# Loading k and q one head at a time, with whole 128-token blocks on the partitions, in an attention and expert kernel

## The chip, the cores and the metric

The kernel runs on one NeuronCore of one Trainium2 chip. The metric is the device time of one execution in microseconds (us). PE is the matrix engine, DVE the vector engine, ACT the scalar engine, POOL the GpSimd engine, and SP the engine whose queue issues most DMAs.

## The reference

Attention with a block-causal mask, followed by a mixture of experts:

```python
B, H, S, D = 8, 8, 576, 64
scores = q @ k.transpose(0, 1, 3, 2) / sqrt(D)
scores = where(pos_q // 64 >= pos_k // 64, scores, -1e9)
attn = softmax(scores); out = attn @ v
x = out.transpose(0, 2, 1, 3).reshape(B * S, H * D)        # 4608 x 512
# 4 groups of 4 experts: the group by argmax(x @ w_group), then the expert in it
y[n] = g_w[n] * e_w[n] * (relu(x[n] @ w1[g, e]) @ w2[g, e])
```

All inputs and the output are float32.

## The kernel before

The attention stage takes two heads of one batch at a time, a pair; there are 32 pairs. Its order is written out by hand: `period(x)` goes through the list ORDER, in which a token names a piece of work (K transposes of k and q, k copies of their high parts, l their low parts, W shifts, P and p copies on POOL, S scores, D row maxima, E exponentials, T and t transposes of the probabilities and their copies, V and v the product with v), and each token belongs to pair x, x+1 or an earlier one. Every engine executes its instructions in the order in which they were issued, and waits in it for semaphores. One pass of the list begins on PE with `K1 V0 K0 S5 K2 S6 T4`.

A pair goes like this. `load` (lines 136 to 147) brings k and q of two heads from HBM to SBUF, with token 4p+c on partition p: one DMA of 256 KB for each of k and q, and one of 32 KB for each one's last 64 tokens (the tail). `prep` transposes them on PE: K0 for k, K1 for q, four transposes each into one PSUM tile (line 174), and K2 for the two tails, two transposes of 64 rows (line 178). Because partition p holds tokens 4p to 4p+3, the four transposed blocks hold interleaved tokens, and `parts` writes them to their places with every fourth word:

```python
f = lambda t: t[:, BLK * z:BLK * z + 512].rearrange("r (p c) -> r c p", c=4)
yield nm, f(hi), f(lo), ps.rearrange("r (c p) -> r c p", c=4)
```

`high` (tokens k0 on ACT, k1 on DVE, k2 on ACT; lines 305 to 311) rounds them to fp32r; `low` (l0, l1, l2 on DVE, line 200) stores the difference. Then three DMAs from SBUF to SBUF on SP's queue (`shift`, line 234; W0, W1, W2) bring rows to the other half of the partitions. W2 overwrites what W0 and W1 read, so it waits until they have landed. Scores with even numbers of the next period read what W2 writes; the first of them is S6. W0 needs k0, k1 and k2, W1 needs l1 and l2.

On SP's queue the order of one period is: the three loads of v (lines 155 and 156), W0, W1, in some periods stores of tokens (line 683), W2, and at the period's end the loads of k and q for the pair three further on. Buffers for k and q are two each, for v three. PSUM tiles of the transposes are taken in turn from two pools of two; T4 takes the buffer that K1 had.

The experts follow after about 400 us: tokens are gathered, weights loaded and split, and two products are formed for each expert slot.

Of the kernel before, what the change touches and what calls it, by code (L numbers as in the profile page):

```python
# [8 lines left out]
F32 = mybir.dt.float32  # L9
# [8 lines left out]
P = 128  # L18
D = 64
S = 576  # L20
BLK = 64
# [55 lines left out]
class Attention:  # L77
# [58 lines left out]
    def load(self, i):  # L136
        nc = self.nc
        b, pr = divmod(i, 4)
        h0 = 2 * pr
        out, src = {}, dict(k=self.k, q=self.q)  # L140
        for nm in "kq":
            out[nm] = self.nat.tile([P, 10, D], F32, tag="nat" + nm, name=f"nat{nm}{i}")
            nc.sync.dma_start(out[nm][:, 0:8, :].rearrange("p (c a) d -> p c a d", a=2),
                              src[nm][b, h0:h0 + 2, 0:512, :].rearrange("a (p c) d -> p c a d", c=4))
        for nm in "kq":
            nc.sync.dma_start(out[nm][0:64, 8:10, :], src[nm][b, h0:h0 + 2, 512:576, :].rearrange("a p d -> p a d"))
        self.lds[i] = out

    def load_v(self, i):
# [9 lines left out]
    def prep(self, i, n):  # L159
        nc = self.nc  # L160
        r = self.rs.setdefault(i, {})
        ld = self.lds[i]
        if "qk" not in r:
            x, t, r["zq"] = r["qk"] = self.qk[i % 2]
            r["ql"], r["q"], r["k"] = x[:, 0, :], [x[:, 1, :], t[:, 0, :]], [x[:, 2, :], t[:, 1, :]]
            r["kl"], r["qm"], r["kn"] = [t[:, 2, :], t[:, 3, :]], [t[:, 4, :], t[:, 5, :]], t[:, 6, :]
            r["qx"] = t[:, 4:6, :].rearrange("p z s -> p (z s)")[:, S - BLK:S + BLK]
        ident = self.c["ident"]
        ps = self.psT(f"tp{i}_{n}")
        r["ps", n] = ps  # L170
        if n < 2:
            x = ld["kq"[n]]
            for c in range(4):
                nc.tensor.transpose(out=ps[:, c * P:(c + 1) * P],  # L174
                                    in_=x[:, 2 * c:2 * c + 2, :].rearrange("p a d -> p (a d)"), identity=ident)
        else:
            for z in range(2):
                nc.tensor.transpose(out=ps[:, 64 * z:64 * z + 64], in_=ld["kq"[z]][0:64, 8:10, :].rearrange("p a d -> p (a d)"),
                                    identity=ident[0:64, 0:64])

    def parts(self, i, n):
        r = self.rs[i]
        ps = r["ps", n]
        for z, nm in enumerate("kq"):
            hi, lo = r[nm][0], r["ql" if nm == "q" else "kn"]
            if n == z:
                f = lambda t: t[:, BLK * z:BLK * z + 512].rearrange("r (p c) -> r c p", c=4)
                yield nm, f(hi), f(lo), ps.rearrange("r (c p) -> r c p", c=4)
            elif n == 2:
                w = slice(0, BLK) if z else slice(512, S)  # L190
                yield nm, hi[:, w], lo[:, w], ps[:, 64 * z:64 * z + 64]
# [1118 lines left out]
```

## Time and profile before

| | |
|---|---|
| median of 3 runs | 921.68 us (920.98 to 924.41) |
| span of the profiled execution, first to last instruction | 926.3 us (4.6 above the median; it has no other time of its own) |
| busy share of the span: PE, DVE, ACT, POOL | 95%, 65%, 58%, 26% |
| PE busy in the stretch 200 to 246 us | 45.9 of 46 |
| DVE and ACT busy in the same stretch | 42.7 and 39.5 of 46 |
| chain that ended last, by engine | PE 73%, DMA 13%, DVE 6%, issue 3%, ACT 2%, POOL 2% |
| largest DMA line of the chain | qk<-qk, 8% |

Busy time of PE counts from the start of an instruction to its modelled end; consecutive ones overlap. The chain follows the last instruction back, at each step to what released it. "Issue" of a DMA is the time on the queue of the engine that starts it; its landing comes later. An engine's idle time is put down to the semaphore that came last.

### The profile page before, as it was taken

To read this page: it belongs to the slowest core of one execution; us is meant where nothing else is said; L and a number is where in the kernel's file an instruction comes from. 1 tells how busy PE (TensorE), PEld (TensorE's weight loads), DVE (VectorE), ACT (ScalarE), POOL (GpSimd) and SP (SyncE) were. 2 spreads that over 40 slices of the span, in tenths; PEclk is the share of its full clock that TensorE was granted. 3 is DMA by queue.
4 is the path that set the end of the run, shared out by engine and by line. 5 is a ranking of instruction groups with operands and counts; after the bars stand their busy time and mean duration, and the time that the engine had idled before them with its cause. 6 is when DMAs were issued, how large, how long until landed. Compare 5 with 4: busy or idle time off the path is not lost.

```text
span 926.3 us, 17222 instructions
## 1 busy us (share of the span) xinstructions
PE 876.0 (95%) x5681; PEld 723.1 (78%) x5681; DVE 601.0 (65%) x1390; ACT 538.2 (58%) x1374; POOL 240.5 (26%) x462
## 2 busy tenths in 40 slices
PE   7899999989997999979989999999999999999996
PEld 5677777777776777757767887887888888988885
DVE  6767988869896888956863435346354465655562
ACT  5888888858885888857333325343243354645451
POOL 5343141312323131314150212321121123122011
PEclk7999999989998999989998999999999999999999
DMA  5777877967788677877442545554564567655671
GB/s 123 147 157 174 181 140 170 162 142 175 140 179 147 151 159 151 183 76 205 100 130 83 161 154 205 173 192 157 169 209 147 151 192 231 209 186 167 175 242 41
DMA packets 192842, 149.03 MB, mean 161 GB/s; under 512 B 127302, under 2 KB 158022, under 8 KB 192752
## 3 DMA queue, kind: packets, MB, share of 16 engines
q1 hardware_dynamic: 184704, 128.17, 56.6%
q0 software_dynamic: 8048, 19.76, 6.2%
q8 instruction: 46, 0.75, 0.3%
q14 instruction: 44, 0.36, 0.2%
HBM read 100.88 MB, written 19.70 MB: 130 GB/s over the span
## 4 chain that ended last, share of the span: by engine, by line
PE 73%; DMA 13%; DVE 6%; issue 3%; ACT 2%; POOL 2%; SPq 0%; POOLq 0%; ACTq 0%; DVEq 0%
PE h L977 17%; PE y L1022 16%; DMA qk<-qk 8%; PE s L254 7%; PE tp L297 7%; PE o L329 6%; PE y L1027 4%; DMA wh<-in_moe_w_dram 2%; PE s L263 2%; PE tp L174 2%; PE h L972 2%; PE ye L1022 2%; DVE nm L268 1%; DVE qk L200 1%; PE xp L945 1%
## 5 line engine op out<-in xcount | busy, mean ns | idle before, releaser
L278 ACT ACTIVATE pb<-s,nm 128x384 f32<-128x384 f32 (+4 forms) x288 | 157.7, 557 | 50.1 <-DVE nm L268 47.0
L268 DVE TENSOR_REDUCE nm<-s 128x1 f32<-128x384 f32 (+4 forms) x288 | 137.7, 512 | 51.4 <-PE s L254 50.3
L254 PE MATMUL s<-qk 128*128 128x384 f32 (+3 forms) x512 | 138.5, 364 | 28.4 <-DMA qk<-qk 19.9
L977 PE MATMUL h<-xt,wh 128*128 128x264 f32 (+6 forms) x704 | 155.3, 312 | 0.0
L929 DVE TENSOR_TENSOR wl<-raw,wh 128x512 fp32r<-128x512 f32 x192 | 123.5, 684 | 10.6 <-ACT wh L928 10.3
L977 PEld LDWEIGHTS h<-xt,wh 128*128 128x128 f32 x704 | 119.4, 188 | 9.1
L309 ACT COPY pt<-tp 128x512 f32<-128x512 f32 (+1 forms) x224 | 113.5, 549 | 16.1 <-PE tp L297 14.9
L297 PE MATMUL tp<-ident,pb 128*128 128x128 f32 x800 | 119.7, 279 | 0.5
L254 PEld LDWEIGHTS s<-qk 128*128 128x128 f32 x512 | 82.2, 198 | 36.1 <-issue 16.9
L977 PE MATMUL h<-xt,wl 128*128 128x264 f32 (+6 forms) x352 | 109.4, 311 | 0.0
L928 ACT CAST wh<-raw 128x512 fp32r<-128x512 f32 x192 | 109.1, 620 | 0.2
L297 PEld LDWEIGHTS tp<-ident,pb 128*128 128x128 f32 x800 | 93.4, 143 | 18.5 <-PE s L254 6.5
L1022 PE MATMUL y<-wh,hring 128*128 128x512 f32 x306 | 107.2, 401 | 0.0
L994 DVE SCALAR_TENSOR_TENSOR hring<-h,hring 128x32 fp32r<-128x32 f32 (+7 forms) x112 | 35.7, 356 | 105.9 <-ACT hring L990 102.6
L329 PE MATMUL o<-pt,vb 128*64 128x320 f32 (+4 forms) x896 | 100.6, 362 | 1.2 <-DVE xte L953 1.0
L990 ACT ACTIVATE hring<-h 128x288 fp32r<-128x288 f32 (+7 forms) x62 | 28.9, 466 | 121.5 <-PE h L977 53.7
L329 PEld LDWEIGHTS o<-pt,vb 128*64 128x64 f32 x896 | 60.3, 137 | 41.0 <-ACT pt L309 2.8
L1048 POOL DMA_INDIRECT out_dram<-ys,ids x40 | 42.4, 1059 | 189.7 <-DVE ys L1044 177.8
L200 DVE SCALAR_TENSOR_TENSOR qk<-tp,qk 128x64 fp32r<-128x64 f32 (+1 forms) x128 | 78.3, 651 | 6.9 <-ACT qk L309 5.7
L892 POOL DMA_INDIRECT xg<-xd,ids x40 | 41.6, 1041 | 104.8 <-DMA ids<-tab 36.4
L977 PEld LDWEIGHTS h<-xt,wl 128*128 128x128 f32 x352 | 66.2, 188 | 1.2
L1022 PEld LDWEIGHTS y<-wh,hring 128*128 128x128 f32 x306 | 57.6, 188 | 11.8
(229 smaller groups left out, 1437.6 us busy)
## 6 DMA issues: line engine op xcount, KB each, us to landing
raw<-in_moe_w_dram SPq DMA_DIRECT2D x96, 512.0 KB, 3.8
qk<-qk SPq DMA_DIRECT2D x93, 288.0 KB, 3.6
natk<-in_k_dram SPq DMA_DIRECT2D x32, 256.0 KB, 4.0
natq<-in_q_dram SPq DMA_DIRECT2D x32, 256.0 KB, 4.7
vb<-in_v_dram SPq DMA_DIRECT2D x64, 128.0 KB, 3.4
xd<-xns SPq DMA_DIRECT2D x32, 256.0 KB, 5.8
wh<-in_moe_w_dram SPq DMA_DIRECT2D x16, 512.0 KB, 4.8
rawe<-in_moe_w_dram SPq DMA_DIRECT2D x8, 512.0 KB, 7.0
```

Source lines behind the costliest of these rows:

```text
L200: nc.vector.scalar_tensor_tensor(out=lo, in0=ps, scalar=0.125 if nm == "q" else 1.0, in1=hi.bitcast(F32), op0=ALU.mult, op1=ALU.subtract)
L254: nc.tensor.matmul(st[:, 0, 0:w], lhsT=r[a][z][:, q0:q0 + P], rhs=r[c][z][:, 0:w], start=x == 0, stop=x == 1)
L268: self.nc.vector.tensor_reduce(out=r["nm"][:, t:t + 1], in_=r["s", t], op=ALU.max, axis=AX.X if t < 8 else AX.XY, negate=True)
L278: nc.scalar.activation(reg, r.pop(("s", t)), AF.Exp, bias=r["nm"][:, t:t + 1], accum_out=self.sms[b][:, pr, t % 2, t // 2:t // 2 + 1])
L297: nc.tensor.transpose(out=o, in_=pb[:, POFF[x] + j * P:POFF[x] + (j + 1) * P], identity=self.c["ident"])
L309: self.nc.scalar.copy(dst, src)
L329: nc.tensor.matmul(o[64 * a:64 * a + 64, BLK * (t - b0):n], lhsT=r["v"][:, a, j, :], rhs=p[:, a], start=x == 0, stop=x == len(pcs) - 1, ti ...
L928: nc.scalar.copy(h[:, sl], s["raw", u][:, sl])
L929: nc.vector.tensor_tensor(out=l[:, sl], in0=s["raw", u][:, sl], in1=h[:, sl].bitcast(F32), op=ALU.subtract)
L977: nc.tensor.matmul(o, lhsT=ww[:, dc, f], rhs=rr[:, dc, t], start=dc == 0 and x == 0, stop=dc == 3 and x == 2)
L1022: nc.tensor.matmul(y[c][0:n], lhsT=hh, rhs=w, start=k == 0 and x == 0, stop=k == 7 and x == 2)
L1048: i = nc.gpsimd.indirect_dma_start(out=self.out, out_offset=bass.IndirectOffsetOnAxis(ap=s["ids"][0:n, c, 0:1], axis=0), in_=ys[0:n], in_o ...
```

## The change

The loads of k and q are made one head at a time, 128 KB each, with token 128c+p on partition p, so that each transposed block holds 128 consecutive tokens. The tails of k and of q go to partitions 0 to 63 and 64 to 127 of the same tile, and one transpose of 128 rows replaces the two of 64. The copies of `parts` become unbroken. The tile of q has 8 instead of 10 rows of 64.

```diff
-        for nm in "kq":
-            out[nm] = self.nat.tile([P, 10, D], F32, tag="nat" + nm, name=f"nat{nm}{i}")
-            nc.sync.dma_start(out[nm][:, 0:8, :].rearrange("p (c a) d -> p c a d", a=2),
-                              src[nm][b, h0:h0 + 2, 0:512, :].rearrange("a (p c) d -> p c a d", c=4))
-        for nm in "kq":
-            nc.sync.dma_start(out[nm][0:64, 8:10, :], src[nm][b, h0:h0 + 2, 512:576, :].rearrange("a p d -> p a d"))
+        for nm, n in (("k", 10), ("q", 8)):
+            out[nm] = self.nat.tile([P, n, D], F32, tag="nat" + nm, name=f"nat{nm}{i}")
+            for a in range(2):
+                nc.sync.dma_start(out[nm][:, a:8:2, :], src[nm][b, h0 + a, 0:512, :].rearrange("(c p) d -> p c d", p=P))
+        for z, nm in enumerate("kq"):
+            nc.sync.dma_start(out["k"][64 * z:64 * z + 64, 8:10, :],
+                              src[nm][b, h0:h0 + 2, 512:576, :].rearrange("a p d -> p a d"))
...
-            for z in range(2):
-                nc.tensor.transpose(out=ps[:, 64 * z:64 * z + 64], in_=ld["kq"[z]][0:64, 8:10, :].rearrange("p a d -> p (a d)"),
-                                    identity=ident[0:64, 0:64])
+            nc.tensor.transpose(out=ps[:, 0:P], in_=ld["k"][:, 8:10, :].rearrange("p a d -> p (a d)"), identity=ident)
...
-                f = lambda t: t[:, BLK * z:BLK * z + 512].rearrange("r (p c) -> r c p", c=4)
-                yield nm, f(hi), f(lo), ps.rearrange("r (c p) -> r c p", c=4)
+                w = slice(BLK * z, BLK * z + 512)
+                yield nm, hi[:, w], lo[:, w], ps
```

## Rows read from the trace of the kernel before

**Rows 1.** Timeline of PE: start us, us, engine line op names [idle before, releaser]
```profile
35.03 0.70 PE L254 MATMUL s<-qk 128*128 128x512 f32 x2 [0.57 <-ACT qk L309]
...
402.49 1.19 PE L254 MATMUL s<-qk 128*128 128x512 f32 x2 [5.62 <-DMA qk<-qk]
```

**Rows 2.** Chain of the stretch 36 to 72 us: start us, us, what
```profile
38.94 4.32 DMA qk<-qk
...
43.40 3.27 DMA qk<-qk
...
46.81 0.71 PE s L254 x2
```

**Rows 3.** Timeline of SP's queue, one period from its loads on
```profile
20.20 0.63 SPq L143 DMA_DIRECT2D natk<-in_k_dram  x1
20.92 0.99 SPq L143 DMA_DIRECT2D natq<-in_q_dram  x1
21.97 0.94 SPq L146 DMA_DIRECT2D natk<-in_k_dram  x1
22.96 0.61 SPq L146 DMA_DIRECT2D natq<-in_q_dram  x1
23.61 1.15 SPq L155 DMA_DIRECT2D vb<-in_v_dram  x2
24.80 0.60 SPq L156 DMA_DIRECT2D vb<-in_v_dram  x1
25.51 1.25 SPq L234 DMA_DIRECT2D qk<-qk  x2
```

**Rows 4.** Timeline of SP's queue, the last period of this kind
```profile
385.61 0.60 SPq L156 DMA_DIRECT2D vb<-in_v_dram  x1
386.32 1.25 SPq L234 DMA_DIRECT2D qk<-qk  x2
```

**Rows 5.** Waits of SP's queue, 20 to 440 us: total us, times, longest us
```profile
SPq L234 <- ACT qk L311: 8.1, 9, 1.4
```

**Rows 6.** Timeline of SP's queue, the longest issue of a load
```profile
182.49 4.99 SPq L146 DMA_DIRECT2D natk<-in_k_dram  x1
```

**Rows 7.** DMA issues by line: count, KB each, median us to landing
```profile
vb<-in_v_dram SPq DMA_DIRECT2D x64, 128.0 KB, 3.4
```

**Rows 8.** Chain of the stretch 108 to 154 us
```profile
108.10 0.27 PE tp L178 x2
...
117.49 0.46 PE tp L174 x4
```

**Rows 9.** Line 178 by form: count, duration ns min/median/max, first and last start
```profile
L178 PEldq EVENT_SEMAPHORE  x31: 51/51/51, 11.3 to 395.3; - x31
```

**Rows 10.** Groups by form: count, busy us, mean ns, idle before, releasers
```profile
L200 DVE SCALAR_TENSOR_TENSOR qk<-tp,qk 128x512 fp32r<-128x512 f32 x64 | 70.1, 1096 | 6.9 <-ACT qk L309 5.7 <-ACT qk L311 0.2
...
L309 ACT CAST qk<-tp 128x512 fp32r<-128x512 f32 x32 | 34.8, 1087 | 7.8 <-PE tp L174 7.2 <-DMA vb<-in_v_dram 0.5
...
L952 ACT CAST xt<-xp 128x512 fp32r<-128x512 f32 x25 | 14.5, 586 | 29.6 <-PE xp L945 29.6
...
L994 DVE SCALAR_TENSOR_TENSOR hring<-h,hring 128x512 fp32r<-128x512 f32 x7 | 4.8, 692 | 13.6 <-ACT hring L990 13.6
```

**Rows 11.** Timeline of all engines around T4 of one period
```profile
203.43 1.10 DVE L200 SCALAR_TENSOR_TENSOR qk<-tp,qk 128x512 fp32r<-128x512 f32 x1
...
204.64 0.31 PEld L297 LDWEIGHTS tp<-ident,pb 128*128 128x128 f32 x3 [0.41 <-PE s L254]
```

**Rows 12.** Chain of the stretch 0 to 37 us
```profile
7.04 1.15 ACT qk L311
...
8.21 1.40 DVE qk L200 x3
...
13.77 1.08 DVE qk L200
```

**Rows 13.** Timeline of POOL around two loads into one tile
```profile
50.87 1.22 POOL L455 DMA_DIRECT2D wcat<-in_moe_w_expert_dram  x2
```

## The prediction

> **What bounds the kernel now.** I read the page's chain first (table above): PE holds 73% of it, and the largest wait by far is DMA qk<-qk, the SBUF-to-SBUF shifts of the attention stage. The change touches only that stage, the first 400 us of the span; the experts after it are PE's work and stay as they are. So I went on to PE's idle time there. PE stands idle visibly in thirteen of the 31 periods, always ahead of the first 512-wide score matmul S6; the first and the last of these are in [rows 1]. The releaser named in the first is an ACT copy, but S6 reads what the third shift (W2) writes. The chain of one of the early stretches says the same [rows 2]: two shifts land at 43.26, W2 is issued at 43.40 and lands 3.27 later, and S6 starts 0.14 behind it. So a period is paced either by PE's own work or by the landing of W2, and the next question is what makes W2 late.
>
> The SP queue answers that [rows 3]. It is in order, and between one W2 and the next W0 stand the loads of k and q, the loads of v and at times a store of tokens. In the shown period W0 goes out at 25.51, 0.11 behind the end of the last v load (24.80 + 0.60). It does so, within 0.11 us of the queue coming free, in 20 of 31 periods; [rows 4] has the last of them. In these the issue times on SP are part of the loop W0, W1, landing, W2, loads, W0. In nine others W0 waited instead for the ACT copy k2, 8.1 us in all [rows 5]: there the compute engines set the pace and SP has slack.
>
> **The change part by part.** *Issues on SP.* Two loads of 256 KB become four of 128 KB; the tails stay two. Today the block takes 23.61 - 20.20 = 3.41 us [rows 3]. The v load already has the new form (128 KB, one head, token 128c+p on partition p): two of them take 24.80 - 23.61 = 1.19, gap included. Four cost 2.38, two tails at 23.61 - 22.96 = 0.65 cost 1.30, two changes of tile 0.14: 3.82 us, or 0.41 more per period. Both ends: at 1.15 for a pair and 0.61 for a tail without gaps, 3.52, so +0.11; at the natk price (20.92 - 20.20 = 0.72) for each half and 0.99 for the first tail, 4.52, so +1.1. I take 0.41, since the v rows are the same operation. Queued behind are the v loads, the stores and W0; W0 delays W1, these W2, and W2 S6. In five of the 20 periods the first tail's issue stands for over 2 us, the longest in [rows 6]: the queue is stuck there on earlier transfers and two more issues should vanish in it. That leaves 15 x 0.41 = **+6.2 us**. The loads are used two periods later, so that their own landing is late by a little costs nothing.
>
> The bytes and the 256-byte pieces are unchanged; a half load lands 3.4 us after its issue [rows 7]. The rows also show that landings overlap: v loads leave 0.6 us apart though each takes 3.4. The Trainium skill, "SBUF — State Buffer", section on the DMA setup-cost knee, says that every transfer pays roughly 2 us that doesn't shrink with its bytes, and to use the largest single transfer; by that rule, if the fixed parts added up in the queue, 62 more DMAs would be an estimated 124 us. The rows just read speak against paying it in series, so the sum goes without it.
>
> *PE.* The two 64-row transposes of the tails take 0.27 of the chain; four full ones take 0.46, so one takes 0.115 [rows 8]: 0.155 saved per period. Against that, K0 and K1 must each wait for two loads instead of one. These landed long before, so only the semaphore instruction counts, 51 ns each [rows 9], if PE's sequencer has no room for it. I take 0.10 (bounds 0.05 and 0.155).
>
> *ACT and DVE copies.* Today they write every fourth word: l0 and l1 on DVE take 1096 ns, k0 on ACT 1087. Unbroken ones of the same size and operation, from PSUM, take 692 (hring) and 586 (xt) [rows 10]. So each DVE instruction saves 0.40 and k0 0.50; with k1 on DVE that is 1.2 us of DVE and 0.5 of ACT per period, some 38 and 16 us in all. Nearly all of it is hidden: by PE where PE paces, by the SP loop where W2 paces. It comes out in two places. The transposes T4 reuse the PSUM buffer of K1, and their weight load sits idle for 0.41 until 204.64, just after l1's end at 203.43 + 1.10 = 204.53 [rows 11]. With l1 done 0.4 to 0.8 earlier that wait goes; part of it lies under S6's stream, so I take 0.25 (bounds 0 and 0.41). And k2 ends earlier, so W0 moves along in the periods that wait for it.
>
> PE-paced periods thus gain 0.10 + 0.25 = 0.35. In the 20 SP-paced ones it only becomes waiting. In the nine where W0 waits for k2 the whole loop moves: 9 x 0.35 = **-3.2 us** (bounds -0.5 and -5.0).
>
> *Start.* Until the loop runs, the copies are serial [rows 12]: ACT 1.15, then DVE 1.40 for l1 and the tails, and before the first row maxima of the next pair the DVE copy k1 and its l1 (1.08). Savings 0.5 + 0.4 + 0.4 + 0.4 = **-1.7 us**. The last halves of the second pair's loads are issued some 1.5 us later than its natq is today; if they bind, only the last 0.8 remains. If the next period's k1 and l1 count too, 2.5. I take 1.7, since the data of the first two pairs is the same.
>
> Sum: 6.2 - 3.2 - 1.7 = +1.3 us, 0.14%. The profiled execution spans 926.3 us, 4.6 above the median of 921.68; its durations are applied as differences, so the forecast is 921.68 + 1.3 = **923.0 us**. Runs of before differ by 3.4 us; 0.5%, 4.6 us, is about what can be told from no change.
>
> **The rivals.** *No change (chance 0.53, 923.0, own range 917.1 to 926.2):* small gains of the compute engines against small losses on SP.
>
> *Slower, by SP issues (0.18, about 930):* each half costs what natk costs today and the first tail stays at 0.99. Halfway to that, +0.9 per period, 15 x 0.9 = 13.5, less 4.9, is +8.6. For it: k and q issues are dearer than v's now. Against: they carry twice the pieces. It decides from about +0.63 per period on (9.5 - 4.9 = 4.6).
>
> *Faster (0.18, about 916.5):* the 0.99 of natq and 0.94 of the tail are what long lists of pieces cost the next issue, and shorter lists give it back. Then +0.11 per period is +1.7, PE's full 0.56 in nine periods is -5.0, the start -1.7 to -2.5: -5.0 to -5.8. For it: the long issues stand directly behind the 256 KB loads. Against: the instruction itself seems to cost 0.5 to 0.6 whatever its size, so six are six.
>
> *The stalls move (0.04 each way, about 917 or 928):* now and then a shift lands so late that PE is idle for up to 5.62 [rows 1]. The loop's phase moves by a us or so; one such stall more or fewer is about 5.
>
> *The halves wait for each other (0.03, about 1130):* the two heads of one tile now lie in alternating slots; if the second load is held until the first has landed, each period has two waits of 3.4 us on SP [rows 7], 31 x 6.8 = 211. Against: on POOL's queue two loads into interleaved columns of one tile go out in 1.22 us together [rows 13]. The setup rule of the Trainium skill named above would be a milder form of this case.
>
> **How the numbers follow.** Faster 0.18 + 0.04 = 0.22; same 0.53; slower 0.18 + 0.04 + 0.03 = 0.25. The range leaves out the serial case and the tails of the others: low 916.5, high 930.0.
>
> **What would show it.** The load block of SP in an unhindered period: 3.8 us against 3.41; below 3.55 the faster rival is right, above 4.05 the slower. k0 near 590 ns, l0 and l1 near 690, and k1 about 0.4 shorter. One transpose of the tails, and no idle weight load ahead of T4. PE's waits for the shifts should grow in number and total (thirteen visible ones now), W0 behind SP's last load in more than 20 periods. The first row maxima of the second pair, which follow the l1 of 13.77 [rows 12], about 1.7 us earlier. Wrong it would be if PE waited for something other than W2, if the halves landed later than v's 3.4, or if the periods paced by k2 did not shrink.

## The result, and the profile after

The change makes the kernel slower: 931.24 us median (926.0 to 935.82) against 920.61 (916.78 to 926.16) for the kernel before on the same chip, a ratio of 1.0135 with a 95% interval of 1.0105 to 1.0165. On another chip it was 927.61 against 911.88, ratio 1.0167 (1.0138 to 1.0195). The forecast was 923.0 with a range from 916.5 to 930.0.

The profiled execution of after took 926.08 us, five below its median. That of before, on which the prediction rests, spans 926.3 us; after took 1.8 more than its span of 924.3, so by the same difference before took an estimated 928, more than any of its ten timed runs here. The two spans therefore say nothing about the change, and before was profiled a second time (913.5 us, below).

The load block first. The timeline of SP's queue in after, one unhindered period, answers to [rows 3] (columns: start us, us, engine, line, operation, names, count):

```profile
104.07 1.55 SPq L144 DMA_DIRECT2D natk<-in_k_dram  x2
105.67 1.33 SPq L144 DMA_DIRECT2D natq<-in_q_dram  x2
107.05 0.63 SPq L146 DMA_DIRECT2D natk<-in_k_dram  x1
107.72 0.62 SPq L146 DMA_DIRECT2D natk<-in_q_dram  x1
108.39 1.14 SPq L156 DMA_DIRECT2D vb<-in_v_dram  x2
109.58 0.61 SPq L157 DMA_DIRECT2D vb<-in_v_dram  x1
110.29 2.07 SPq L233 DMA_DIRECT2D qk<-qk  x2
```

From the first half of k to the first load of v it is 108.39 - 104.07 = 4.32; the median over the periods is 4.10, with most at 4.07 to 4.11. Before it was 3.41 in [rows 3], with a median of 3.45. W0 goes out directly behind SP's last load in 26 of the 30 periods.

The copies answer to [rows 10]. Groups of after by form (count, busy us, mean ns, idle before with releasers):

```profile
L199 DVE SCALAR_TENSOR_TENSOR qk<-tp,qk 128x512 fp32r<-128x512 f32 x64 | 43.9, 686 | 6.0 <-ACT qk L308 4.8 <-ACT qk L310 0.2
...
L308 ACT CAST qk<-tp 128x512 fp32r<-128x512 f32 x32 | 19.2, 601 | 6.0 <-PE tp L175 5.3 <-DMA natq<-in_q_dram 0.2 <-DMA vb<-in_v_dram 0.2
```

1096 and 1087 ns became 686 and 601. In the chain of the start, the l1 that stood at 13.77 [rows 12] now begins at 12.56:

```profile
12.56 0.69 DVE qk L199
13.25 0.47 DVE nm L267
```

So the compute engines got what the change promises. The page of after shows where it went (busy times; then the chain that ended last by engine and by line):

```profile
PE 864.5 (94%) x5649; PEld 721.3 (78%) x5649; DVE 572.2 (62%) x1390; ACT 522.8 (57%) x1374; POOL 239.8 (26%) x462
...
PE 73%; DMA 17%; DVE 4%; issue 4%; SPq 1%; ACT 1%; POOL 0%; POOLq 0%; DVEq 0%; ACTq 0%
PE h L976 17%; PE y L1021 16%; DMA qk<-qk 14%; PE s L253 7%; PE tp L296 7%; PE o L328 6%; PE y L1026 4%; PE s L262 3%; PE h L971 2%; PE tp L175 2%; PE ye L1021 2%; DMA wh<-in_moe_w_dram 2%; PE xp L944 2%; PE xn L672 2%; PE he L976 1%
```

The shifts, qk<-qk, are 14% of the chain against 8% before. To see in which periods, I count a period from the start of K1 on PE to the next K1: thirty, the first from about 9 us on. With four pairs to a batch, the stores of tokens and four of a batch's five token scatters (indirect DMAs of POOL into the table, Z1, Z2, Z3, Z0 in ORDER, 8 bytes a row) come at the end of periods 10, 14, 18, 22 and 26; periods 11, 15, 19, 23 and 27 lie behind them. All times in us, one profiled execution each:

| kernel | first period | the five behind a batch | the other 24 | K1 of period 31 starts |
|---|---|---|---|---|
| before, first profile | 11.9 | 82.7 | 290.6 | 394.2 |
| before, second profile | 12.0 | 75.0 | 287.9 | 383.8 |
| after, first profile | 9.9 | 94.2 | 281.8 | 394.8 |
| after, second profile | 10.0 | 95.4 | 282.0 | 396.4 |

Between the two second profiles (913.5 and 926.97 us, on two chips on which before takes 912) the change gains 2.0 in the first period and 5.9 in the 24, and loses 20.4 in the five: 12.6 in all by period 31. It wins in the ordinary periods and loses in five places. The sizes are those of single executions: the five of before differ by 7.7 us between its two profiles, and against the first one the loss is 11.5 to 12.7. The win in the 24 leans on the stalls, too: when these are taken away ("After without the scatters", below), the 24 take 290.0.

One of the five, in after: SP's queue; POOL's scatters; the chain; PE's timeline with idle time before an instruction; and the windows of the period and two parts of it (us; busy us with counts of PE, its weight loads, DVE, ACT and POOL; granted clock of PE; DMA share; GB/s).

```profile
129.08 0.60 SPq L233 DMA_DIRECT2D qk<-qk  x1
129.77 1.55 SPq L144 DMA_DIRECT2D natk<-in_k_dram  x2
131.38 1.14 SPq L144 DMA_DIRECT2D natq<-in_q_dram  x2
132.56 2.33 SPq L146 DMA_DIRECT2D natk<-in_k_dram  x1
134.93 2.57 SPq L146 DMA_DIRECT2D natk<-in_q_dram  x1
```

```profile
124.77 1.02 POOL L801 DMA_INDIRECT tab<-pay,pi  x1 [0.17 <-POOL mark L800]
...
128.63 0.96 POOL L801 DMA_INDIRECT tab<-pay,pi  x1 [0.23 <-issue]
```

```profile
129.08 8.73 DMA qk<-qk
```

```profile
137.95 1.19 PE L253 MATMUL s<-qk 128*128 128x512 f32 x2 [5.11 <-DMA qk<-qk]
```

```profile
128.82:150.78 21.96, 15.71 (x106) 12.10 (x106) 9.94 (x21) 11.46 (x34) 2.93 (x5) 0.84 0.84 127
128.82:138.00 9.18, 2.93 (x22) 1.79 (x21) 2.47 (x5) 3.78 (x13) 1.76 (x4) 0.87 1.02 95
138.00:142.00 4.00, 4.00 (x14) 3.37 (x15) 1.55 (x4) 1.15 (x3) 1.17 (x2) 0.50 0.81 171
```

W2 goes out at 129.08, half a us behind the issue of the fourth scatter, and lands 8.73 later; an unhindered one takes 3.4 to 3.6 in the chain of this profile. Meanwhile the DMA engines are busy throughout (1.02) but move only 95 GB/s. PE waits 5.11 us in one piece for it, and then runs 4 us at the lower of its two clock levels (granted clock 0.50, 1.2 GHz): S6's two matmuls take 1.19 instead of 0.70. The queue behind W2 is stuck as well (2.33 and 2.57 for 32 KB tails, otherwise 0.63).

### The profile page after: what moved, and what is told of

It is laid out like the page before. It is cut to its first block, busy times and chain, and to the rows that moved or that the text cites. A ratio compares the mean times of both kernels' runs of the same rounds, so it can differ in the third digit from the quotient of the medians.

```text
span 924.3 us, 17206 instructions
## 1 busy us (share of the span) xinstructions
PE 864.5 (94%) x5649; PEld 721.3 (78%) x5649; DVE 572.2 (62%) x1390; ACT 522.8 (57%) x1374; POOL 239.8 (26%) x462
## 4 chain that ended last, share of the span: by engine, by line
PE 73%; DMA 17%; DVE 4%; issue 4%; SPq 1%; ACT 1%; POOL 0%; POOLq 0%; DVEq 0%; ACTq 0%
PE h L976 17%; PE y L1021 16%; DMA qk<-qk 14%; PE s L253 7%; PE tp L296 7%; PE o L328 6%; PE y L1026 4%; PE s L262 3%; PE h L971 2%; PE tp L175 2%; PE ye L1021 2%; DMA wh<-in_moe_w_dram 2%; PE xp L944 2%; PE xn L672 2%; PE he L976 1%
## 5 line engine op out<-in xcount | busy, mean ns | idle before, releaser
L267 DVE TENSOR_REDUCE nm<-s 128x1 f32<-128x384 f32 (+4 forms) x288 | 141.5, 516 | 83.2 <-PE s L253 64.2
L253 PE MATMUL s<-qk 128*128 128x384 f32 (+3 forms) x512 | 134.9, 360 | 34.6 <-DMA qk<-qk 28.7
L928 DVE TENSOR_TENSOR wl<-raw,wh 128x512 fp32r<-128x512 f32 x192 | 123.5, 684 | 10.6 <-ACT wh L927 10.3
L308 ACT COPY pt<-tp 128x512 f32<-128x512 f32 (+1 forms) x224 | 113.1, 550 | 16.2 <-PE tp L296 11.5
L296 PEld LDWEIGHTS tp<-ident,pb 128*128 128x128 f32 x800 | 95.3, 143 | 14.3 <-DVE tmp L710 3.4
L1021 PE MATMUL y<-wl,hring 128*128 128x512 f32 x153 | 60.5, 395 | 0.0
```

The lines of the kernel that those rows point to most:

```text
L253: nc.tensor.matmul(st[:, 0, 0:w], lhsT=r[a][z][:, q0:q0 + P], rhs=r[c][z][:, 0:w], start=x == 0, stop=x == 1)
L267: self.nc.vector.tensor_reduce(out=r["nm"][:, t:t + 1], in_=r["s", t], op=ALU.max, axis=AX.X if t < 8 else AX.XY, negate=True)
L296: nc.tensor.transpose(out=o, in_=pb[:, POFF[x] + j * P:POFF[x] + (j + 1) * P], identity=self.c["ident"])
L308: self.nc.scalar.copy(dst, src)
L928: nc.vector.tensor_tensor(out=l[:, sl], in0=s["raw", u][:, sl], in1=h[:, sl].bitcast(F32), op=ALU.subtract)
L1021: nc.tensor.matmul(y[c][0:n], lhsT=hh, rhs=w, start=k == 0 and x == 0, stop=k == 7 and x == 2)
```

## The experiments

Ratios are to the kernel before on the same chip, with a 95% interval. Line numbers follow each kernel.

### The issues

**One DMA a tensor in the new layout.** The kernel after, but:

```diff
-            for a in range(2):
-                nc.sync.dma_start(out[nm][:, a:8:2, :], src[nm][b, h0 + a, 0:512, :].rearrange("(c p) d -> p c d", p=P))
+            nc.sync.dma_start(out[nm][:, 0:8, :], src[nm][b].rearrange("h s d -> (h s) d")[h0 * S:h0 * S + 1024, :]
+                              .rearrange("(c p) d -> p c d", p=P))
```

> The changed kernel with k and q again in one 256 KB DMA each (four issues per period as before), the tails and the unbroken copies as changed. For the address pattern's sake the second head's tokens are read 64 too early, so this kernel computes other scores with the same amount of work. Theory (the two added issues per period lengthen SP's loop): the load block falls back from 4.08 to about 3.4 us, the periods that wait for k2 or PE stay at 10.9, and the time is 5 to 9 us below before (ratio 0.990 to 0.995). Rival (the pattern of 128 consecutive tokens, or the token scatter's stalls, cost the time): still 8 to 12 us above before (1.009 to 1.013).

0.996 (0.9931 to 0.9989). The timeline of SP's queue has four issues again, and the block is 3.47 long:

```profile
100.09 0.55 SPq L143 DMA_DIRECT2D natk<-in_k_dram  x1
100.69 1.09 SPq L143 DMA_DIRECT2D natq<-in_q_dram  x1
101.82 1.03 SPq L146 DMA_DIRECT2D natk<-in_k_dram  x1
102.89 0.62 SPq L146 DMA_DIRECT2D natk<-in_q_dram  x1
103.56 1.27 SPq L156 DMA_DIRECT2D vb<-in_v_dram  x2
```

The same layout, copies and tails gain 0.4% with two issues fewer. The five periods take 83.7, the other 24 279.8: against after, 10.5 and 2.0 less. The 83.7 are still 8.7 above the second profile of before, though no issue was added, and 1.0 above the first.

**The split alone.** The kernel before with one head a DMA, still token 4p+c, copies with every fourth word, two tail transposes:

```diff
-            nc.sync.dma_start(out[nm][:, 0:8, :].rearrange("p (c a) d -> p c a d", a=2),
-                              src[nm][b, h0:h0 + 2, 0:512, :].rearrange("a (p c) d -> p c a d", c=4))
+            for a in range(2):
+                nc.sync.dma_start(out[nm][:, a:8:2, :], src[nm][b, h0 + a, 0:512, :].rearrange("(p c) d -> p c d", c=4))
```

> The kernel before with nothing but the split: k and q one head a DMA, token 4p+c on partition p as before, strided copies and two tail transposes kept. Theory (issues on SP): all of the loss and none of the gains, 10 to 18 us above before (1.011 to 1.020), load block near 4.1 us. Rival (pattern of 128 consecutive tokens or the shared tail is what costs): same as before within 0.3%.

1.0268 (1.0226 to 1.031), above the range expected; the block is 4.37, the five periods take 87.4, the other 24 297.0. Without the fast copies the issues cost 12.4 us in the five and 9.1 in the 24, against the second profile of before.

**Two more issues with nothing in them.** The kernel before plus:

```diff
+        extra = self.nat.tile([1, 2, D], F32, tag="extra", name=f"extra{i}")
+        for a in range(2):
+            nc.sync.dma_start(extra[:, a, :], src["k"][b, h0 + a, 0:1, :])
```

> The kernel before with its own layout, its two 256 KB loads and its two tail transposes, and two more loads of 256 bytes each per period, into a tile that nothing reads, issued on SP behind the tails. If the issues themselves are the cost (the instruction stands on SP whatever its bytes): the load block grows from 3.4 us to about 4.5 (two times 0.55), W0 stands directly behind SP's last load in over 25 of 30 periods, and the time is 1.5 to 3 per cent above before, as with the split alone (1.027). If the cost came with the splitting of the bytes (more but shorter lists, later landings), these 31 KB in all cost nothing: block below 3.8, ratio below 1.005.

1.0214 (1.0169 to 1.0259). SP's queue in one period:

```profile
105.07 0.63 SPq L143 DMA_DIRECT2D natk<-in_k_dram  x1
105.80 1.00 SPq L143 DMA_DIRECT2D natq<-in_q_dram  x1
106.84 0.77 SPq L146 DMA_DIRECT2D natk<-in_k_dram  x1
107.66 0.61 SPq L146 DMA_DIRECT2D natq<-in_q_dram  x1
108.32 0.74 SPq L149 DMA_DIRECT2D extra<-in_k_dram  x2
```

Two loads of 256 bytes stand 0.74 us on SP, less than the 1.1 expected, and cost 2.1%. W0 goes out directly behind SP's last load in 20 periods, not in over 25; seven waits of the shifts on SP, 3.7 us in all, are put down to loads of k and q that had to land. The bytes and the shape of the pieces are not the cost; the number of DMAs issued is. Against the second profile of before the five periods take 12.3 more and the other 24 4.1 more: most of the loss sits behind the batches here too.

**The shared tail transpose alone.** The kernel before with the tails of after and their one transpose:

> The kernel before with the shared tail transpose alone: both tails in one tile, one 128-row transpose, loads and copies of the main part as before. Theory: SP's block stays at 3.4 us, a PE-paced period shortens by 0.1 to 0.2 us, the time by 0 to 3 us (0.997 to 1.000). Rival (a tail loaded to partitions 64 to 127 lands later or costs DMA time): above before by 0.3% or more.

0.9946 (0.9911 to 0.9981), better than expected. On PE's timeline the transposes of the tails and S6 in the second profile of before, then in this kernel:

```profile
93.23 0.27 PE L178 MATMUL tp<-ident,natk 64*128 64x64 f32 x1
93.34 0.22 PE L178 MATMUL tp<-ident,natq 64*128 64x64 f32 x1
93.49 0.73 PE L254 MATMUL s<-qk 128*128 128x512 f32 x2
```

```profile
93.01 0.27 PE L178 MATMUL tp<-ident,natk 128*128 128x128 f32 x1
93.04 0.71 PE L253 MATMUL s<-qk 128*128 128x512 f32 x2
94.07 0.52 PE L296 MATMUL tp<-ident,pb 128*128 128x128 f32 x3 [0.32 <-DVE qk L199]
```

S6 starts 0.03 after the start of the one transpose, not 0.26 after that of the first of two, and K1 to S6 takes 2.21 instead of 2.53. T4 then waits 0.32 for the slow l1, so a PE-paced period stays at 11.5: this saving needs the fast copies to come out. What the kernel gains lies elsewhere: 2.5 us in the five periods (72.5) and 2.2 in the other 24 (285.7), with PE waiting 8.2 us in four places for the shifts instead of 10.1 in six. Both differences are smaller than those between the two profiles of before (7.7 and 2.7).

### Moving the loads of v

**After with the v loads behind W1.** SP waits there for W0 and W1 to land anyway:

```diff
-        if 0 <= x - 1 < N:
-            self.load_v(x - 1)
+        vdone = False
...
             self.token(x - lag(tok), tok, N)
+            if not vdone and tok == ("W", 1):
+                vdone = True
+                if 0 <= x - 1 < N:
+                    self.load_v(x - 1)
```

> The changed kernel with the three loads of v moved on SP's queue from ahead of W0 to behind W1, where the queue stands waiting for W0 and W1 to land. Theory (SP's loop paces): 1.8 us leave the loop, W0 again waits for k2 in most periods, periods without router work near 10.9 us, and the time is 10 to 25 us below the changed kernel, 3 to 15 below before (0.984 to 0.997). Rival (the stalls after the token scatter pace, or the transfers themselves): no better than the changed kernel, 1.008 or more.

0.9971 (0.9937 to 1.0005), against 1.0135 without the move. W0 waits for k2 (0.02 to 0.04 behind its end) in 21 periods instead of 3, and the other 24 periods fall to 271.6. The five stay at 89.6: freeing SP does not cure those. The shifts W2 in front of them go out 0.7 to 3.0 us ahead of K1, as in before (0.5 to 3.8), and still land late, 7.5 to 8.9 us after their issue (the chain):

```profile
118.03 8.93 DMA qk<-qk
...
169.63 8.09 DMA qk<-qk
```

**The same move in the kernel before.**

> The kernel before, with only the v loads issued behind W1 and not ahead of W0. If SP's loads between W2 and W0 pace before too, as the loop of the prediction has it, this shortens the loop by about 2 us: W0 waits for k2 in nearly all periods, the sum of the stalls ahead of S6 falls below 15 us, and the ratio is 0.985 to 0.995. If the move helps only because the new layout had lengthened the loop, before gains nothing: 0.997 to 1.003.

1.0079 (1.0045 to 1.0112), outside both expectations. W0 waits for k2 in 25 periods and the waits of PE are short, as the loop theory says, but the time rises.

**Shared tails and the move, neither split nor fast copies.**

> The kernel before with the shared transpose of the tails and the v loads behind W1, and neither the split nor the unbroken copies. Against the same kernel with the unbroken copies and the split (0.997): if the faster copies are worth their 0.6 to 0.7 us in a period that PE paces, this one should be slower than that, 1.000 or more. If what they give is lost again in the stalls behind each router batch and in the two more issues, this one is as fast or faster: 0.990 to 0.995, with PE-paced periods still at 11.5 to 11.6.

1.0108 (1.0066 to 1.0151): the move loses again. The reason showed later, in all kernels with it: the loads of v for the last two pairs go out late too, and PE waits for them. PE's timeline in the spread kernel with the move (below):

```profile
399.33 1.08 PE L328 MATMUL o<-pt,vb 128*64 128x256 f32 x2 [6.02 <-DMA vb<-in_v_dram]
```

From the last score to the last product with v, before takes 13.5 us (second profile), these kernels 20.4 to 23.2.

**After with the v loads on POOL's queue** (`nc.gpsimd` in place of `nc.sync` in `load_v`).

> The kernel after with the three v loads on POOL's queue, ahead of everything that POOL does in the period. SP then issues only six loads between W2 and W0, 4.1 us. If SP's issues are all that costs the change its gain, W0 waits for k2 in most periods, PE-paced periods stay at 10.9, and the ratio is 0.985 to 0.995. If POOL is held up by issuing (over 1 us each there) its copies of k and q come late and the score matmuls wait for POOL: 1.00 or more.

0.9974 (0.9945 to 1.0004), the same as behind W1 and between the two expectations, with the five at 88.4. The Trainium skill, "DMA: Bandwidth & Descriptors", section "Issuing engines are not separate DMA queues", says that another issuing engine saves only the sequencer's time, usually small beside the transfer itself. The runs agree with the first half. That time, some 0.6 us for a load of v against a landing of 3.4, is what decides here: nine loads stand in the queue of one period, and two more of 256 bytes cost 2.1%.

### The scatters

**After without the scatters of the first five batches.**

```diff
     def scatter(self, b, st, c):
         n = TQN[c]
+        if b < EBAT - 1:
+            return
```

> The kernel after without the token scatters of the first five batches (25 of 40: table rows of 8 bytes, written from POOL; so the experts gather the empty row for those tokens and write fewer rows of the output, and only the attention stage may be compared). If the late shift after each batch comes from these scatters (they are issued between W1 and 1.5 us after W2), W2 lands 3.5 to 5.5 us after its issue in the batch periods 10, 14, 18 and 22 too, no wait of PE ahead of S6 is above 4.5 us there, and the four periods 11, 15, 19, 23 take about 13 us each instead of 22.0, 18.2, 19.9 and 16.7. If it comes from the 256 KB stores of the tokens or from the loads, these stay at 16 to 20.

The whole kernel ran at 0.9946 (0.9922 to 0.9971), but only the attention stage counts. Periods 11, 15, 19 and 23 take 13.7, 13.0, 14.2 and 13.9 instead of 22.0, 18.2, 19.9 and 16.7. The window of period 11:

```profile
128.41:142.09 13.68, 13.20 (x106) 10.34 (x106) 9.81 (x21) 10.93 (x33) 2.16 (x4) 1.00 0.71 155
```

DMA share 0.71 in place of 0.84, clock 1.00 in place of 0.84. The W2 in front of period 11 lands 3.04 us after its issue, not 8.73 (the chain):

```profile
127.44 3.04 DMA qk<-qk
```

The stores of 256 KB are still there, so the scatters make the late shift. Part comes back: the other 24 take 290.0, 8.2 more than in after and 2.1 more than in the second profile of before, with W0 directly behind SP in 29 of 30 periods. The SP loop is then the next bound.

**The last four scatters of a batch spread over four periods.** Three kernels: after; after with v behind W1; before. The edit in ORDER is the same:

```diff
-... E1 E3 Z1:6 Z2:6 Z3:6 Z0:6
+... E1 E3 Z1:6 Z2:7 Z3:8 Z0:9
```

> The kernel after with the four last scatters of a batch one in each of four periods and not four in a row. If four in a row make the stall after each batch, and one alone is covered by the slack of W2 (which lands 1.5 to 2 us before S6 needs it in a period that PE paces), the periods after a batch fall from about 18 to 13 to 15, which is 15 to 20 us in all: ratio to before 0.99 to 1.00. If the stall has another cause, no change: 1.010 to 1.017, as after.

> The same spread scatters in the kernel after with the v loads behind W1 (0.997). By the scatter theory the sum of the waits ahead of S6 falls from 22 to under 8 us and the ratio to 0.975 to 0.985; it should then beat both kernels. By the rival (stores and loads) no change, 0.995 to 1.000.

> The same spread scatters in the kernel before. It tells what of the gain belongs to the spreading alone. By the scatter theory before gains too, since it has waits of 7 us in periods 15 and 23: 0.985 to 0.995. If the change's faster copies come out only once these waits are gone, the distance of the kernel after with both edits to this one is 2 us per four periods, 0.8 to 1 per cent.

After 1.0067 (1.0038 to 1.0097), less than was expected, the five at 83.4, the others back at 291.0. With v behind W1 0.9836 (0.981 to 0.9861), the five at 74.4, the others at 275.6: as expected. Before 0.9908 (0.9878 to 0.9938), the five at 72.5, the others at 289.1. So there are two causes behind one stall: the scatters make a shift late, and SP's loop cannot make up for it. Either cure alone leaves the other.

**The tails with spread scatters, and before with both edits.**

> The kernel before with the shared transpose of the tails and the spread scatters: none of the split, none of the unbroken copies. If the split and the unbroken copies are worth more than their two issues once the stalls behind the batches are gone, it is slower than the kernel after with v behind W1 and spread scatters (0.984): 0.988 to 0.995. If the shared transpose and the spreading were all that there was to win, it is as fast: 0.980 to 0.986.

> The kernel before with v behind W1 and the spread scatters. It differs from the 0.984 kernel by exactly the change (layout and shared tail transpose). If the change's own work gain is the 0.6 to 0.7 us per PE-paced period read from the traces, about 27 such periods are 17 us: this kernel is at 1.000 to 1.005. If v behind W1 made the kernel before slower (1.008) for a reason that spreading removes, it is at 0.985 to 0.992, and the change is worth little even there.

0.9909 (0.9882 to 0.9936) and 1.0013 (0.9978 to 1.0048). The first has the shortest five, 69.9. The second differs from the 0.9836 kernel by exactly the change.

**Second profiles of before and after.**

> The kernel before, unchanged, for a second profile of it: the first profiled execution took about 928 us against a median of 921.7 and 920.6. If its waits of 7 us in periods 15 and 23 are part of every execution, they stand here again and the attention stage is at 385 us. If they belong to that execution, the waits behind the batches sum to less, by 5 to 10 us, the stage is at 373 to 380, and the prediction's sum started from a baseline with more SP-paced periods than usual.

> The kernel after, unchanged, for a second profile of it beside the second one of before, on the kind of chip where before takes about 913 us. If the waits behind the batches are what the change costs on every chip, the five periods 11, 15, 19, 23 and 27 take 88 to 96 us again (before 75.0), the other 24 take 280 to 284 (before 287.9), and the ratio is 1.010 to 1.017. If the first profile of after was an outlier like the first of before, the five take under 85 us.

Their periods stand in the table above. The window of period 11 in before, and PE's largest wait from 20 to 395 us in before and in after (total us, times, longest):

```profile
126.77:141.48 14.71, 13.55 (x107) 10.46 (x107) 10.89 (x21) 11.89 (x34) 2.16 (x4) 1.00 0.60 103
```

```profile
PE s L254 <- DMA qk<-qk: 10.1, 6, 4.7
```

```profile
PE s L253 <- DMA qk<-qk: 22.3, 10, 4.8
```

From K1 to S6 the first profile of before had 7.0 and 7.4 in periods 15 and 23; the second has 6.5 and 3.4. Its long stretches behind the batches belong in part to that one execution. Those of after come back in both of its profiles, on two chips.

**The best version, and its twin in the layout of before.** v behind W1, but at the head of the period for the last two pairs; spread scatters:

```diff
-        vdone = False
+        vdone = x > N - 2
+        if vdone:
+            self.load_v(x - 1)
```

> The kernel after with the v loads behind W1 and the spread scatters (0.984), but the v loads of the last two pairs at the head of their period again. In the 0.984 kernel, and in every one with v behind W1, these last loads go out 2 to 4 us later, PE waits 6.0 and 6.2 us for them, and the stretch from the last score to the last product of the values takes 20 to 23 us in place of 13.5 to 14.5. If that is a side effect of the move alone, the stretch is back at about 14 us and the ratio is 0.974 to 0.979, the fastest kernel of the study. If the stretch is long for another reason, 0.982 to 0.986.

> The same edits of the order (v behind W1 but for the last two pairs, spread scatters) in the kernel before, so that it differs from the previous one by exactly the change. By the reading of the traces the layout and the shared transpose are then worth 0.6 to 0.7 us in each of some 20 to 27 periods that PE paces, 13 to 18 us: ratio 0.990 to 0.996, 1.5 to 2 per cent above the other. If the change is worth nothing once SP and the scatters are out of the way, both are equal within 0.5 per cent.

0.9755 (0.9714 to 0.9795), 891.75 us, the fastest of the study, and 0.995 (0.9923 to 0.9977) for the twin without the change. From the last score to the last product with v it takes 14.1 and 14.3. The chain of the faster one:

```profile
PE 82%; DMA 9%; DVE 4%; issue 2%; ACT 1%; SPq 1%; POOLq 0%; ACTq 0%; DVEq 0%
PE h L981 17%; PE y L1026 17%; PE tp L296 9%; PE s L253 9%; PE o L328 8%; DMA qk<-qk 5%; PE y L1031 4%; PE tp L175 3%; PE s L262 3%; PE h L976 2%; DMA wh<-in_moe_w_dram 2%; PE xn L677 2%; PE ye L1026 2%; PE xp L949 2%; PE lg L695 1%
```

With SP and the scatters out of the way the change is worth 0.995 - 0.9755, about 2%: in the 24 periods 286.6 - 273.4 = 13.2 us, in the first 2.2, while the five differ by 2.1 the other way. These are 13.3 of the 16.7 us between the medians; the rest lies behind period 31.

## Why the prediction was wrong

The bound was named rightly: the SP loop of loads, W0, W1, landing and W2. Two loads of 256 bytes in that loop cost more than the whole change (1.0214 against 1.0135). The rival "slower, by SP issues", put at 0.18 and about 930, was the case. It was to decide from +0.63 per period; between the medians of the two profiles 4.10 - 3.45 = 0.65 was measured, and 4.10 is above the bound of 4.05 that the text had set for it. That its 930 comes so near to 931.24 is luck: it had +0.9 in each of 15 ordinary periods, a first tail at 0.99 (0.63 was measured) and, like the forecast, nothing in the other five.

**The step that failed** is "In five of the 20 periods the first tail's issue stands for over 2 us ... two more issues should vanish in it". These five are the stretches behind the batches, and there the change lost 20.4 us by the second profiles (11.5 by the first), priced at nothing. The two issues by themselves, with nothing else changed, lost 12.3 there (the two tiny loads) and 12.4 (the split alone), against the second profile of before. The row on which the step rested [rows 6] showed SP stuck behind late transfers. It did not show that SP had slack: W2 of that stretch is itself late, and all that delays it ends on PE. That the scatters hold up the shifts is shown by leaving them out.

How the change makes it worse is only in part seen. In both profiles of after W2 goes out later against PE, from 1.4 us ahead of K1 to 2.1 behind it in the five places, where in both of before it went out 0.5 to 3.8 ahead; so a late landing costs PE more. It also falls behind more of the scatters: in the second profile of before, W2 goes out 0.3 to 2.6 us ahead of the fourth scatter in each batch, in that of after 0.2 to 4.5 us behind it in four of five. This order alone does not explain the late landing: with v behind W1, W2 is 0.5 to 2.3 us ahead of the fourth scatter in four of five places, and the shifts still take 7.5 to 8.9 us. What share of the loss belongs to the issues and what to the faster copies (the five take 83.7 with these and no added issue) stays open.

**A term that was too small**: 0.41 per period for the issues. The v rows gave 1.19 for a pair; the k halves take 1.55 and the q halves 1.11 to 1.33. The instruction is the same as v's; its place in the queue, directly behind W2, is not. No run shows that the place is the reason.

**A gain that was too small**: 0.35 in a PE-paced period. It is 0.60, 0.74 and 0.65 (11.53, 11.60 and 12.68 became 10.93, 10.86 and 12.03). The shared transpose gives 0.32 in place of 0.10, since S6 stood behind both small ones; what is left of the first, 0.28, comes with the end of T4's wait, in place of 0.25. In after:

```profile
94.82 0.27 PE L178 MATMUL tp<-ident,natk 128*128 128x128 f32 x1
94.85 0.71 PE L253 MATMUL s<-qk 128*128 128x512 f32 x2
95.40 0.49 PE L296 MATMUL tp<-ident,pb 128*128 128x128 f32 x3
```

The transposes T4 follow with no wait, as foreseen in [rows 11]. The gain also reached more than the nine periods that were counted for it: 12 of the 24 in the first profile of after have these short lengths, and in front of nine of them W0 went out directly behind SP's last load. That W0 stands behind SP does not yet make a period SP-paced, as the prediction counted. Because of this the other 24 periods came out 5.9 us faster, where the sum had them 6.2 - 3.2 = 3.0 slower; that hid part of the error that mattered.

**What held**: the start (2.0 against 1.7); k0 at 601 and l0, l1 at 686 ns (590 and 690); one transpose for the tails; W0 behind SP in 26 periods (21 in the second profile of before); more waits of PE for the shifts (22.3 us against 10.1). The setup rule of the Trainium skill ("SBUF — State Buffer", the DMA setup-cost knee), an estimated 124 us for 62 more DMAs paid in series, was rightly left out. The loss is 10.6 to 15.7 us, and the expectation that halves wait for each other showed nowhere: the two of k are out in 1.55 us, those of q in 1.11 to 1.33.

The first profile of before was a poor base for counting which periods wait for what: its five periods took 82.7 us and those of the second 75.0.

## What to carry to other kernels

On an in-order queue that a loop runs through, count issues and not bytes: two loads of 256 bytes per period cost this kernel 2.1%. A stretch in which a queue stands still need not be a cover for more work on it; ask what late event it waits for and whether the new work makes that event later. When a change of work gains in every ordinary period and the total loses, split the periods by kind, cure the place of the loss, and time the change again: it was +1.35% before the cure and -2% after it.

## What was not expected of the hardware

- Four scatters of 128 rows of 8 bytes, 4 KB in all, go with DMA engines that are busy but move little (share 1.02 at 95 GB/s over 9.2 us, with loads queued behind them), and a shift issued behind them lands after 8.7 us. Without them the same 9.2 us show a share of 0.81 at 178 GB/s, and that shift lands after 3.0. Spread over four periods they cost less.
- PE's clock. Behind a wait of 5.11 us in period 11, one of 2.83 in period 19 and one of 2.34 in period 15 (with 1.13 shortly before), S6 ran at the lower level (granted clock 0.50), 1.19 us in place of 0.70; behind one of 3.34 in period 27 of the same execution it did not (granted clock 1.00). Where it fell, the way from S6 to the next K1 took 12.1 to 13.0 us in place of 10.7, a second price of the same late shift.
- A DMA of 256 bytes stands 0.37 us on SP's queue (two in 0.74), one of 32 KB 0.6, one of 128 KB 0.57 to 0.78 (half of the pairs), one of 256 KB 0.55 to 1.09: from the first to the last the bytes grow a thousandfold and the price on the queue at most threefold.
